# PSUM tiles of one bank from the experts on, and a new order of splits, scans and decodings

## The chip, the cores and the metric

The kernel runs on one core of a Trainium2 chip. The metric is the device time of one execution in microseconds (us), the median of three runs. The profile is of one more execution, taken by the hardware profiler. TensorE (PE) multiplies, VectorE (DVE), ScalarE (ACT) and GpSimd (POOL) do the rest, SyncE (SP) issues most of the loads. Each engine takes its instructions strictly in the order of the program and waits at an instruction until what it needs is there.

## The reference

Three layers follow each other on 2 x 768 tokens of width 512 (attention has 8 heads of 64).

```python
# 1 linear attention with decay
for t in range(S):
    state = gamma * state + einsum('bhd,bhe->bhde', k[:, :, t], v[:, :, t])
    y[:, :, t] = scale * einsum('bhd,bhde->bhe', q[:, :, t], state)
# 2 mixture of 8 experts, 512 -> 1024 -> 512
fresh_e = argmax(logits[b, s])
e = fresh_e if s == 0 or local_gate[b, s] < 0.5 else prev_e
out[b, s] = softmax(logits[b, s])[e] * (maximum(x[b, s] @ w1[e], 0) @ w2[e])
# 3 feed-forward with a convolution of three taps along the tokens
h = maximum(x @ w_in, 0)
conv_out = sum of conv_w[k] * (h shifted by k - 1)
out = (h * sigmoid(conv_out)) @ w_out
```

The weights of the third layer arrive as 64-bit floats, two 32-bit words each.

## The kernel before

The program is in the order in which the code emits it (a manual schedule); nothing sorts it afterwards. Waits between engines are set by tile: an instruction that writes into a tile waits until the earlier readers of that tile are done, whichever part of it they read.

**PSUM.** Eight banks of 128 x 512 floats. `xp`, `sc` and `x` are tiles of two banks each, `rt` and `state` of one. From the experts on the banks are handed out in rings: ring a is the two halves of `xp`, ring b the two halves of `sc` and then `rt`, ring c the two halves of `x`. `bank(ring)` gives the next one.

**Attention** works on 12 tiles of 128 tokens. Step i runs a_Z, a_AV(i), a_S(i+1) (scores, L335, masked by VectorE in L340), a_U, a_X(i) (L394, the output and the router's logits) and a_store. Spread between these are: the parts of the router, `route(g)` for five groups of tiles (codes turned by L454, a scan over tokens in L456 that holds the previous expert, back transposes in L463, counts in L470, slots in L496); the splitting of the first weights, and the decoding of the first weights of the third layer.

**Splitting.** A weight tile of 128 x 1024 (`raw`) is split in two parts, whose sum is exact: ScalarE copies it to a short type (`whi`, L174, split_first) and VectorE takes the difference (`wlo`, L182, split_second). Each product is then three matmuls: hi x hi, lo x hi, hi x lo. `split_unit` does both halves.

**Decoding.** `draw` is half a weight tile of 64-bit words. dec_load issues its DMA, dec_first lets ScalarE read it twice (L214, L215), then five VectorE operations (L217 to L223) and two of GpSimd (L225, L226) make `wdec`; dec_part runs one of these stages, dec_second all that are left, and then issues the next load.

**Experts.** Expert 0 and 7 are done in two halves of 128 tokens by `alone(e, half)` (L641 first product, ScalarE's relu `hr` L652, transposes back in L629, L660 second product, `ys` out by L670 and L671). Experts 1 to 6 are done with 256 tokens at once: L1 (L694) fills four banks (two of `sc`, `rt`, `state`) in four rounds dt; in the last round each bank, once full, is read by ScalarE (`hh`, L699) and by VectorE (`hl`, L700). T (L572) transposes the tokens of the next expert into ring a, read by ScalarE (`xsh`) and VectorE (`xsl`, L575); L2 (L723) is the second product. Between the two halves of expert 0 stands `overflow`, a branch (L816) that all engines read.

**Third layer.** c_T (L929) transposes the experts' output, six tiles a batch. h2 (L972) makes 32 blocks of 386 columns, which ScalarE reads as `hs` (L986); three taps in L989 and L991, the gate in L995 to L1001 (`gh`, `gl`). o2 (L1024) is the last product, copied out as `os` (L1038, L1047).

Of the kernel before, what the change touches and what calls it, by code (L numbers as in the profile page):

```python
# [8 lines left out]
F32 = mybir.dt.float32  # L9
# [5 lines left out]
ALU = mybir.AluOpType  # L15
AX = mybir.AxisListType
# [7 lines left out]
P = 128  # L24
# [16 lines left out]
Z_LT_HALF = -1.5 * 2.0 ** -23  # L41

WBUFS = 10
DEC_STEPS = (8, 10)
RAW_STEP = 2
SPLIT_STEPS = (4, 5, 6, 7, 8, 9, 10, 11)


def _float_of(bits):
# [51 lines left out]
def tile_kernel(ctx: ExitStack, tc: tile.TileContext, consts, qk, kv, w1, w2, w_in, conv_w, w_out, out):  # L101
# [15 lines left out]
    xrow = scr[0:YROW, :]  # L117

    psp = ctx.enter_context(tc.tile_pool(name="psp", bufs=1, space=PSUM))
    xp2, sc2, x2 = (psp.tile([P, 2, 512], F32, name=n) for n in ("xp", "sc", "x"))  # L120
    rtb, std = (psp.tile([P, 512], F32, name=n) for n in ("rt", "state"))
    rings = {"a": [xp2[:, 0], xp2[:, 1]], "b": [sc2[:, 0], sc2[:, 1], rtb], "c": [x2[:, 0], x2[:, 1]]}

    def bank(ring):
        rings[ring].append(rings[ring].pop(0))
        return rings[ring][-1]
# [119 lines left out]
    def dec_first(pool=None):  # L246
        dec_second()
        u = dnx["run"]
        if u >= len(dec_src):
            return  # L250
        dnx["run"] += 1
        dec_raw["g"] = decode(dec_raw.pop(u), wdec[u // 2][:, (u % 2) * DM:(u % 2 + 1) * DM], pool)
        next(dec_raw["g"])

    def dec_part():
        if "g" in dec_raw and next(dec_raw["g"], 0) == 0:
            dec_raw.pop("g")
            dec_load()

    def dec_second(queue=nc.sync):  # L260
        if "g" in dec_raw:
            for _ in dec_raw.pop("g"):
                pass
            dec_load(queue)
# [62 lines left out]
    def a_S(i, ps=range(NP)):  # L327

        if ps[0] == 0:
            sc_t[i] = sc2  # L330
        sc = sc_t[i]
        for p in ps:
            for j in range(2):
                o = j * D
                nc.tensor.matmul(sc[:, j, p * P:(p + 1) * P], lhsT=qk_t[i][o:o + D, p // 2, 1, p % 2, :],  # L335
                                 rhs=qk_t[i][o:o + D, p // 2, 0, p % 2, :], start=True, stop=True)
        if ps[-1] < NP - 1:
            return
        A_t[i] = at.tile([P, 2 * NP, P], F32, name="A", tag="A", bufs=1)
        nc.vector.tensor_tensor(out=A_t[i], in0=sc.rearrange("p j (a t) -> p (j a) t", a=NP),  # L340
                                in1=cv("mask").unsqueeze(1).to_broadcast([P, 2 * NP, P]), op=ALU.mult)
# [3 lines left out]
    def a_Z(i):  # L345

        xp = xp_t[i] = xp2
        if i % NC:
            z = Z[(i % NC - 1) % 2]
            for p in range(NP):  # L350
                for j in range(2):
                    o, a = slice(j * D, (j + 1) * D), slice(p % 2 * D, (p % 2 + 1) * D)
                    nc.tensor.matmul(xp[a, j, p // 2 * P:(p // 2 + 1) * P], lhsT=z[o, p * D:(p + 1) * D],
                                     rhs=qk_t[i][o, p // 2, 0, p % 2, :], start=(p < 2), stop=False,
                                     skip_group_check=True)
# [32 lines left out]
    def a_X(i):  # L388

        xT = xT_t.pop(i)  # L390
        x_t[i] = x2[:, 0], x2[:, 1]
        for p in range(NP):
            o = (p % 2) * P
            nc.tensor.matmul(x_t[i][p // 2][:, o:o + XN], lhsT=xT[:, p, :], rhs=xw[:, p, :],  # L394
                             start=(p % 2 == 0), stop=(p % 2 == 1), skip_group_check=True)
# [28 lines left out]

    def logits(i):

        nc.vector.tensor_reduce(out=LG[:, i, :], in_=x2[:, :, P:XN].rearrange("p m e -> p e m"), axis=AX.X, op=ALU.add)

    def route(g):

# [76 lines left out]
    def part(i):  # L507
        if i in rts:
            next(rts[i], None)
# [69 lines left out]
    def first_gather():  # L579

        st = st_t["st"][:, NP * D:NP * D + 4 * E]
        ve = nc.vector
        ve.tensor_copy(perm, st[:, 0:2 * E])
        ve.tensor_tensor(out=perm0, in0=perm[:, 0:1], in1=st[:, 2 * E:2 * E + 1], op=ALU.add)
        nc.gpsimd.indirect_dma_start(out=x0, out_offset=None, in_=scr[0:1 + FIRST * P, :],
                                     in_offset=bass.IndirectOffsetOnAxis(ap=perm0, axis=0))

    def first_T():
        xs0[:] = [dp.tile([P, KD, P], F32R, name="xs0", tag=tag) for tag in ("ds", "df")]
        transposed(x0, *xs0)  # L590

    def moe(mo):
# [141 lines left out]

        first = alone(0, 0, False)
        g3, g4 = len(GROUPS) - 2, len(GROUPS) - 1
        part(g3)
        rts[g4] = route(g4)
        part(g4)
        next(first)  # L740
        next(first)
        part(g4)
        next(first)
# [12 lines left out]
        for n, _ in enumerate(first):  # L756
            if n in (1, 4):
                next(blocks, None)
            if n in (3, 5):
                split_unit(nc.vector)  # L760
            if n >= 5:
                next(rest, None)
            if n == 5:
                T(0, (1,))
# [309 lines left out]
    with tc.manual_schedule():  # L1074
        a_load_qk(0, 2)
        nc.scalar.dma_start(out=tq.rearrange("p a n -> p (a n)"), in_=consts[:, 0:n0])
        nc.scalar.dma_start(out=C, in_=consts[:, n0:])
        a_load_kv(0)
        a_load_qk(1)
        a_load_kv(1)  # L1080
        a_load_qk(2)
        a_load_kv(2)
        nc.vector.memset(x_last, 0.0)
        keep_warm(10)
        nc.vector.memset(small_zero, 0.0)
        nc.gpsimd.memset(ones, 1.0)
        sloti = x0.bitcast(I32)[:, 0:CAP]
        nc.gpsimd.iota(sloti, pattern=[[1, CAP]], base=1, channel_multiplier=0)
        nc.gpsimd.tensor_copy(slot1, sloti)
        for half in range(2):  # L1090
            a_scale_q(0, nc.vector, slice(half, half + 1))
            a_S(0, range(NP)[half * NP // 2:(half + 1) * NP // 2])
        a_scale_v(0, nc.gpsimd)
        a_scale_q(1, nc.vector)
        nc.sync.dma_start(out=scr[0:1, :], in_=x_last[0:1].rearrange("p a t -> p (a t)"))
        for i in range(NT):
            if i == 0:
                gate = C[:, n_wg:n_wg + KD * (E + 1)].rearrange("p (k e) -> p k e", k=KD)
                for odd in range(2):
                    o = (E + 1) * odd  # L1100
                    nc.gpsimd.tensor_copy(xw[:, odd::2, o:o + P], ident.unsqueeze(1).to_broadcast([P, KD // 2, P]))
                    o = P if odd == 0 else 0
                    nc.gpsimd.tensor_copy(xw[:, odd::2, o:o + E + 1], gate[:, odd::2, :])
                nc.gpsimd.tensor_copy(tri, cv("mask"))
                nc.gpsimd.tensor_copy(sel, ident[:, P - 1:P].to_broadcast([P, P]))
                a_scale_v(1, nc.gpsimd)
            ends = {b: g for g, (a, b) in enumerate(GROUPS)}
            late, due, done = ends.get(i - 1), ends.get(i), ends.get(i + 1)
            a_Z(i)
            part(late)  # L1110
            a_AV(i)
            a_load_qk(i + 3)
            a_scale_q(i + 2, nc.gpsimd)
            part(late)
            if i + 1 < NT:
                a_S(i + 1)
            dec_part()
            a_U(i)
            a_load_kv(i + 3)
            a_scale_v(i + 2, nc.gpsimd)  # L1120
            dec_part()
            part(due)
            if i in SPLIT_STEPS:
                split_first()
            if i == NT - 1:
                first_T()
                part(due)
            part(late)
            if i == FIRST + 1:
                first_gather()  # L1130
            a_X(i)
            logits(i)
            a_store(i)
            if done is not None and i < NT - 1:
                rts[done] = route(done)
                part(done)
            dec_part()
            if i == DEC_STEPS[0] - 2:
                dec_load()
                dec_load()  # L1140
            if i in DEC_STEPS:
                dec_first()
            if RAW_STEP <= i and nxt["load"] < 4:
                load_unit()
            if i in SPLIT_STEPS:
                split_second(nc.vector)
        att.close()
        with ExitStack() as c2:
            mo = c2.enter_context(tc.tile_pool(name="mo", bufs=1))
            moe(mo)  # L1150
        dst.close()
        with ExitStack() as c3:
            fo = c3.enter_context(tc.tile_pool(name="fo", bufs=1))
            moe2(fo)
# [34 lines left out]
```

## Time and profile before

| | |
|---|---|
| median of three runs | 500.0 us (498.72 to 502.33) |
| profiled execution | 500.29 us |
| its span on the core | 498.5 us, 1.8 us less |
| mean granted clock of TensorE | 0.938 |

The profile's page lists the busy time of each engine, then groups of instructions. The list of waits gives for TensorE, by line, what it waited for, in us over the span, how often, and the longest. A timeline row has the start and the length of an instruction or a run of like ones, and in brackets the idle time of its engine ahead of it with what ended that. The table of stretches has the busy time of each engine between two times. A granted clock of 1.00 is 2.4 GHz, and 0.50 is 1.2 GHz.

### The profile page before, as it was taken

What the parts mean: (1) busy time and instruction counts of PE and PEld (TensorE: products, weight loads), DVE (VectorE), ACT (ScalarE), POOL (GpSimd) and SP (SyncE); (2) the same over time, 40 slices, a digit from 0 to 9 for tenths busy, and PEclk for the clock granted to TensorE, in tenths of its full rate; (3) what the DMA queues carried; (4) which work ended last, traced back from release to release, by engine and by line L of the source; (5) the groups of instructions that cost most, each with busy time, mean ns of one, the idle gap of its engine ahead of it and who ended that gap; (6) DMA issues with size and microseconds to landing.
All of it is one profiled execution on the core that took longest, in us unless ns stands there. A gap on an engine that the chain in (4) does not pass through costs nothing. (4 is left out here: it accounts for less than half of the span.)

```text
span 498.5 us, 7286 instructions
## 1 busy us (share of the span) xinstructions
PE 425.0 (85%) x2772; PEld 361.7 (73%) x2772; DVE 293.6 (59%) x484; ACT 243.5 (49%) x445; POOL 169.2 (34%) x142
## 2 busy tenths in 40 slices
PE   7998677789797896969798859868898979998996
PEld 4887565568686795968778747648886858986875
DVE  3478685628695665757556653556980632893250
ACT  2455451337463465555536441556863523773241
POOL 4544442301436072453616061603840200441020
PEclk9999877979998799999889997969999998999999
DMA  8999754536678376675928120311301001000101
GB/s 322 309 352 409 281 186 149 149 107 227 218 237 307 99 263 207 223 268 178 316 99 279 59 86 0 113 36 43 107 0 43 21 21 44 1 0 21 43 0 63
DMA packets 27718, 73.36 MB, mean 147 GB/s; under 512 B 2837, under 2 KB 3221, under 8 KB 27682
## 3 DMA queue, kind: packets, MB, share of 16 engines
q1 hardware_dynamic: 17634, 48.37, 27.4%
q0 software_dynamic: 4000, 13.66, 9.4%
q10 hardware_dynamic: 6048, 10.85, 5.8%
q8 instruction: 22, 0.36, 0.3%
q14 instruction: 14, 0.11, 0.1%
HBM read 62.39 MB, written 10.49 MB: 146 GB/s over the span
## 5 line engine op out<-in xcount | busy, mean ns | idle before, releaser
L182 DVE TENSOR_TENSOR wlo<-raw,whi 128x1024 fp32r<-128x1024 f32 x64 | 84.7, 1335 | 39.7 <-ACT whi L174 39.7
L174 ACT CAST whi<-raw 128x1024 fp32r<-128x1024 f32 x64 | 66.4, 1051 | 38.3 <-PE x L723 24.3
L996 POOL TENSOR_TENSOR sg<-sg,hs 128x384 f32<-128x384 f32 x32 | 35.4, 1105 | 114.6 <-ACT sg L995 114.5
L991 DVE SCALAR_TENSOR_TENSOR cs<-hs,cw,cs 128x384 f32<-128x384 f32 x64 | 48.2, 753 | 43.0 <-ACT cs L989 41.7
L225 POOL TENSOR_TENSOR dmf<-dmf,ds 128x512 f32<-128x512 f32 x14 | 28.1, 2008 | 127.4 <-DVE ds L223 93.6
L972 PE MATMUL sc<-x,whi 128*128 128x386 f32 x168 | 38.2, 349 | 6.4 <-ACT hs L986 6.4
L1024 PE MATMUL x<-whi,gh 128*128 128x512 f32 x88 | 36.4, 413 | 6.9 <-ACT os L1038 6.9
L694 PE MATMUL sc<-xsh,whi 128*128 128x256 f32 x96 | 28.1, 292 | 14.2 <-DVE hl L700 14.2
L723 PE MATMUL x<-whi,hh 128*128 128x512 f32 x96 | 39.0, 407 | 0.0
L723 PE MATMUL x<-wlo,hh 128*128 128x512 f32 x96 | 38.4, 400 | 0.0
L972 PEld LDWEIGHTS sc<-x,whi 128*128 128x128 f32 x168 | 30.1, 193 | 9.4 <-ACT hs L986 9.3
L1024 PE MATMUL x<-whi,gl 128*128 128x512 f32 x88 | 35.3, 402 | 0.0
L1024 PE MATMUL x<-wlo,gh 128*128 128x512 f32 x88 | 35.3, 401 | 0.0
L1001 DVE TENSOR_TENSOR gl<-sg,gh 128x384 fp32r<-128x384 f32 x32 | 29.2, 911 | 4.6 <-ACT gh L1000 4.6
L723 PE MATMUL x<-whi,hl 128*128 128x512 f32 x96 | 30.1, 395 | 0.0
L694 PEld LDWEIGHTS sc<-xsh,whi 128*128 128x128 f32 x96 | 18.6, 194 | 15.7 <-DVE hl L700 15.4
L226 POOL TENSOR_TENSOR wdec<-dmf 128x512 f32<-128x512 f32 x14 | 28.7, 2049 | 1.1
L694 PE MATMUL sc<-xsh,wlo 128*128 128x256 f32 x96 | 27.4, 286 | 0.0
L694 PE MATMUL sc<-xsl,whi 128*128 128x256 f32 x96 | 27.4, 285 | 0.0
L1024 PEld LDWEIGHTS x<-whi,gh 128*128 128x128 f32 x88 | 16.9, 192 | 13.0 <-ACT os L1038 9.6
L600 POOL DMA_INDIRECT xg<-scr,permi x15 | 18.2, 1214 | 20.6 <-DVE up L523 11.0
L340 DVE TENSOR_TENSOR A<-sc,C 128x1024 f32<-128x1024 f32 x12 | 14.7, 1223 | 13.5 <-PE sc L335 13.5
(217 smaller groups left out, 1055.1 us busy)
## 6 DMA issues: line engine op xcount, KB each, us to landing
raw<-in_moe_w_dram SPq DMA_DIRECT2D x64, 512.0 KB, 4.6
kv<-in_kv_dram SPq DMA_DIRECT2D x12, 512.0 KB, 7.3
qk<-in_qk_dram SPq DMA_DIRECT2D x11, 512.0 KB, 6.9
scr<-ys ACTq DMA_DIRECT2D x16, 256.0 KB, 5.6
draw<-in_moe_w_out_dram POOLq DMA_DIRECT2D x8, 512.0 KB, 5.0
scr<-xo ACTq DMA_DIRECT2D x11, 256.0 KB, 6.5
out_dram<-os ACTq DMA_DIRECT2D x11, 256.0 KB, 2.0
draw<-in_moe_w_in_dram SPq DMA_DIRECT2D x4, 512.0 KB, 7.3
```

Source lines behind the costliest of these rows:

```text
L174: nc.scalar.copy(hi, raw[u])
L182: engine.tensor_tensor(out=lo, in0=t, in1=hi.bitcast(F32), op=ALU.subtract)
L225: nc.gpsimd.tensor_tensor(out=f, in0=f, in1=s.bitcast(F32), op=ALU.mult)
L226: nc.gpsimd.tensor_tensor(out=out, in0=f, in1=a.bitcast(F32), op=ALU.add)
L600: nc.gpsimd.indirect_dma_start(out=t, out_offset=None, in_=xrow, in_offset=bass.IndirectOffsetOnAxis(ap=permi[:, col:col + 1], axis=0))
L694: nc.tensor.matmul(o, lhsT=a[:, fs], rhs=b_[:, dt, :], start=(dt == 0 and n == 0 and ft % 2 == 0), stop=(dt == KD - 1 and n == 2), skip_gr ...
L723: nc.tensor.matmul(yp[t], lhsT=a[:, ft, t * P:(t + 1) * P], rhs=b_[:, ws], start=(ft == 0 and a is hh and b_ is wh), stop=(ft == KF - 1 an ...
L972: nc.tensor.matmul(pb[:, 0:WN], lhsT=split[u_in + dt][wi][:, fs], rhs=x_[dt // 2][:, dt % 2, :], start=(n == 0), stop=(n == 3 * KD - 1))
L991: nc.vector.scalar_tensor_tensor(out=cs, in0=tap[j], scalar=cw[:, j, ft:ft + 1], in1=cs, op0=ALU.mult, op1=ALU.add)
L996: nc.gpsimd.tensor_tensor(out=sg, in0=sg, in1=tap[1], op=ALU.mult)
L1001: nc.vector.tensor_tensor(out=gl, in0=sg, in1=gh.bitcast(F32), op=ALU.subtract)
L1024: nc.tensor.matmul(ops[t][:, 0:n_], lhsT=a[:, ts_], rhs=b_[:, ws], start=(ft == 0 and n == 0), stop=(ft == KF - 1 and n == 2))
```

## The change

Tiles of two banks live in a pool of their own until the last attention step; then that pool is closed, and another with six tiles of one bank each is opened, from which the rings take `a0`, `a1`, `b0`, `b1` (and `rt`), `c0`, `c1`. X of the last attention tile is the first to write there, so its logits are a copy and an addition. Only unit 0 is decoded within attention, with its load issued at the end of step 7 in place of 6; unit 1 is decoded in alone(0,0). Tile 9 has no split any more, which alone(0,0) takes over, and at steps with no due route part VectorE's half of the split comes ahead of the router's logits. Code transposes and scan of a route group stand right behind S, back transposes and comparisons after X, counts after the next AV. The route of the last group begins in the last attention step, and the first transposes of the experts come behind X(11).

```diff
-DEC_STEPS = (8, 10)
+DEC_STEPS = (8,)
-SPLIT_STEPS = (4, 5, 6, 7, 8, 9, 10, 11)
+SPLIT_STEPS = (4, 5, 6, 7, 8, 10, 11)
...
-    xp2, sc2, x2 = (psp.tile([P, 2, 512], F32, name=n) for n in ("xp", "sc", "x"))
     rtb, std = (psp.tile([P, 512], F32, name=n) for n in ("rt", "state"))
-    rings = {"a": [xp2[:, 0], xp2[:, 1]], "b": [sc2[:, 0], sc2[:, 1], rtb], "c": [x2[:, 0], x2[:, 1]]}
+    pst = ExitStack()
+    psa = pst.enter_context(tc.tile_pool(name="psa", bufs=1, space=PSUM))
+    xp2, sc2, x2 = (psa.tile([P, 2, 512], F32, name=n) for n in ("xp", "sc", "x"))
+    rings = {}
...
-        x_t[i] = x2[:, 0], x2[:, 1]
+        x_t[i] = (x2[:, 0], x2[:, 1]) if i < NT - 1 else (bank("c"), bank("c"))
...
+        else:
+            nc.vector.tensor_copy(LG[:, i, :], x_t[i][0][:, P:XN])
+            nc.vector.tensor_tensor(out=LG[:, i, :], in0=x_t[i][1][:, P:XN], in1=LG[:, i, :], op=ALU.add)
...
         g3, g4 = len(GROUPS) - 2, len(GROUPS) - 1
+        next(first)
         part(g3)
-        rts[g4] = route(g4)
-        part(g4)
-        next(first)
         next(first)
...
-            if n in (3, 5):
+            if n == 2:
+                dec_first()
+            if n == 6:
+                dec_second()
+            if n in (0, 3, 5):
                 split_unit(nc.vector)
...
             a_Z(i)
-            part(late)
             a_AV(i)
             a_load_qk(i + 3)
             a_scale_q(i + 2, nc.gpsimd)
             part(late)
-            if i + 1 < NT:
+            if not last_tile:
                 a_S(i + 1)
+            part(due)
             dec_part()
             a_U(i)
             a_load_kv(i + 3)
             a_scale_v(i + 2, nc.gpsimd)
-            dec_part()
-            part(due)
+            if late is not None and due is None:
+                part(late)
+            if i == FIRST + 1:
+                first_gather()
             if i in SPLIT_STEPS:
                 split_first()
-            if i == NT - 1:
-                first_T()
-                part(due)
-            part(late)
-            if i == FIRST + 1:
-                first_gather()
+                if due is None:
+                    split_second(nc.vector)
+            if last_tile:
+                pst.close()
+                ps = ctx.enter_context(tc.tile_pool(name="ps", bufs=1, space=PSUM))
+                for n, ring in enumerate("abc"):
+                    rings[ring] = [ps.tile([P, 512], F32, name=f"{ring}{j}") for j in range(2)]
+                rings["b"].append(rtb)
             a_X(i)
             logits(i)
             a_store(i)
-            if done is not None and i < NT - 1:
+            if done is not None:
                 rts[done] = route(done)
                 part(done)
+            part(due)
+            if last_tile:
+                first_T()
             dec_part()
-            if i == DEC_STEPS[0] - 2:
+            if i == DEC_STEPS[0] - 1:
                 dec_load()
                 dec_load()
```

Three places show what moves. On TensorE, at the end of L1 of expert 3, T for expert 4 and the start of L2, with the semaphores that an instruction waits for. Before:

```order
L694 MATMUL state<-xsl,whi 128x256
L572 MATMUL xp<-C,xg 128x128 [waits DMASW4_49]
L572 MATMUL xp<-C,xg 128x128 x3
L572 MATMUL xp<-C,xg 128x128 [waits DMASW5_49,DVE_49]
L572 MATMUL xp<-C,xg 128x128 x3
L723 MATMUL x<-whi,hh 128x512 [waits Activation_49]
```

and after:

```order
L700 MATMUL state<-xsl,whi 128x256
L578 MATMUL a_982<-C,xg 128x128 [waits DMASW4_49]
L578 MATMUL a_982<-C,xg 128x128 x3
L578 MATMUL a_981<-C,xg 128x128 [waits DMASW5_49]
L578 MATMUL a_981<-C,xg 128x128 x3
L729 MATMUL c_986<-whi,hh 128x512 [waits Activation_49]
```

The order is the same; the second group of transposes no longer waits for VectorE, only for its own load.

On SP, the loads issued in steps 6 to 8 of attention. Before:

```order
L302 DMA qk<-in_qk_dram 128x1024
L309 DMA kv<-in_kv_dram 128x1024
L243 DMA draw<-in_moe_w_in_dram 128x1024 x2
L165 DMA raw<-in_moe_w_dram 128x2x512
L302 DMA qk<-in_qk_dram 128x1024
L309 DMA kv<-in_kv_dram 128x1024
```

and after:

```order
L304 DMA qk<-in_qk_dram 128x1024
L311 DMA kv<-in_kv_dram 128x1024
L167 DMA raw<-in_moe_w_dram 128x2x512
L304 DMA qk<-in_qk_dram 128x1024
L311 DMA kv<-in_kv_dram 128x1024
L167 DMA raw<-in_moe_w_dram 128x2x512
L245 DMA draw<-in_moe_w_in_dram 128x1024 x2
```

The two draws, ahead of a raw tile and of qk and kv of tile 10 before, stand behind these and the next raw tile after.

On VectorE, steps 8 and 9 of attention (`A` is the masked scores of tile 9, `far` the scan of the third group). Before:

```order
L182 TENSOR_TENSOR wlo<-raw,whi 128x1024
L340 TENSOR_TENSOR A<-sc,C 128x1024
L217 TENSOR_SCALAR dmag<-dmag 128x512
L218 TENSOR_SCALAR dmag<-dmag 128x512
L220 TENSOR_SCALAR ds<-draw 128x512
L221 SCALAR_TENSOR_TENSOR dmag<-dmag,ds 128x512
L223 TENSOR_SCALAR ds<-dmag 128x512
L456 SCALAR_TENSOR_TENSOR far<-C,far,rt 1x384
L427 TENSOR_REDUCE LG<-x 128x9
```

and after:

```order
L342 TENSOR_TENSOR A<-sc,C 128x1024
L462 SCALAR_TENSOR_TENSOR far<-C,far,rt 1x384
L219 TENSOR_SCALAR dmag<-dmag 128x512
L220 TENSOR_SCALAR dmag<-dmag 128x512
L430 TENSOR_REDUCE LG<-x 128x9
L471 TENSOR_SCALAR mi<-rt 128x3
L472 TENSOR_TENSOR OH<-mi,C 128x24
L473 TENSOR_TENSOR OHT<-OH,C 128x24
L222 TENSOR_SCALAR ds<-draw 128x512
L223 SCALAR_TENSOR_TENSOR dmag<-dmag,ds 128x512
L225 TENSOR_SCALAR ds<-dmag 128x512
```

The scan moved ahead of the decoding, whose last three operations moved behind the logits and the comparisons of the route.

## Rows read from the trace of the kernel before

**Rows 1.** The page's first part: busy time, share of the span, instructions.

```profile
PE 425.0 (85%) x2772; PEld 361.7 (73%) x2772; DVE 293.6 (59%) x484; ACT 243.5 (49%) x445; POOL 169.2 (34%) x142
```

**Rows 2.** Waits of TensorE: line, what it waited for, us, times, longest.

```profile
PE sc L694 <- DVE hl L700: 14.2, 6, 3.5
PE xp L572 <- DVE xsl L575: 9.1, 6, 1.6
PE x L1024 <- ACT os L1038: 6.9, 7, 2.3
PE sc L972 <- ACT hs L986: 6.4, 9, 1.3
PE sc L641 <- ACT hr L652: 6.0, 2, 5.4
PE xp L929 <- DVE x L942: 5.4, 5, 1.5
...
PE sc L641 <- ACTq L816: 2.8, 1, 2.8
```

**Rows 3.** Timeline of one wait in expert 4, all engines.

```profile
215.50 1.23 DVE L182 TENSOR_TENSOR wlo<-raw,whi 128x1024 fp32r<-128x1024 f32 x1 [1.65 <-ACT whi L174]
...
216.64 0.68 DVE L700 SCALAR_TENSOR_TENSOR hl<-sc,hh 128x512 fp32r<-128x512 f32 x1
...
217.38 0.39 PE L694 MATMUL sc<-xsh,whi 128*128 128x256 f32 x1 [2.28 <-DVE hl L700]
```

**Rows 4.** Stretches: alone(0,1), experts, c_T and h2, o2, h2.

```profile
core 0: us, PE busy (x) PEld busy (x) DVE busy (x) ACT busy (x) POOL busy (x), PEclk, DMA share, GB/s
100.00:106.00 6.00, 5.40 (x13) 4.25 (x14) 0.00 (x0) 0.00 (x0) 0.94 (x1) 0.50 0.45 132
158.00:168.00 10.00, 8.12 (x32) 7.24 (x33) 4.23 (x7) 4.29 (x7) 0.67 (x1) 0.50 0.38 134
189.73:217.38 27.65, 23.79 (x152) 21.43 (x153) 18.27 (x24) 15.02 (x20) 12.50 (x9) 1.00 0.68 229
248.00:253.00 5.00, 3.60 (x14) 2.82 (x13) 2.18 (x5) 2.71 (x4) 0.00 (x0) 0.50 0.31 117
321.00:336.00 15.00, 9.59 (x40) 6.59 (x40) 8.81 (x20) 7.88 (x19) 2.54 (x3) 0.75 0.24 68
328.80:338.00 9.20, 7.54 (x24) 5.96 (x25) 4.43 (x9) 4.13 (x10) 0.00 (x0) 0.50 0.00 1
410.50:413.70 3.20, 3.20 (x8) 2.52 (x9) 0.00 (x0) 0.00 (x0) 0.00 (x0) 0.50 0.24 84
423.96:445.62 21.66, 19.79 (x108) 18.84 (x108) 18.85 (x27) 17.20 (x36) 9.39 (x9) 1.00 0.00 1
```

**Rows 5.** Timeline of ScalarE at loads that are decoded, experts 2 and 7.

```profile
154.43 0.66 ACT L214 ACTIVATE dmf<-draw 128x512 f32<-128x512 f32 x1 [4.84 <-DMA draw<-in_moe_w_in_dram]
...
296.48 0.66 ACT L214 ACTIVATE dmf<-draw 128x512 f32<-128x512 f32 x1 [2.98 <-DMA draw<-in_moe_w_out_dram]
```

**Rows 6.** Attention from step 6 on: timeline, and the page's row of such loads.

```profile
39.05 1.87 SPq L243 DMA_DIRECT2D draw<-in_moe_w_in_dram  x2
...
43.76 0.42 SPq L302 DMA_DIRECT2D qk<-in_qk_dram  x1
...
55.02 1.76 PE L335 MATMUL sc<-qk 64*128 64x128 f32 x16 [2.17 <-POOL qk L316]
...
57.96 0.42 DVE L217 TENSOR_SCALAR dmag<-dmag 128x512 f32<-128x512 f32 x1
...
62.07 0.99 DVE L456 TENSOR_TENSOR_SCAN far<-C,far,rt 1x384 f32<-1x384 f32 x1
...
63.12 0.48 PE L463 MATMUL rt<-C,far 1*128 1x1 f32 x3 [2.83 <-DVE far L456]
...
76.21 0.37 PE L463 MATMUL rt<-C,far 1*128 1x1 f32 x2 [1.20 <-DVE far L456]
draw<-in_moe_w_in_dram SPq DMA_DIRECT2D x4, 512.0 KB, 7.3
```

More of the change, by code (lines that the diff above doesn't have):

```diff
@@ L425, in logits @@
     def logits(i):
-        nc.vector.tensor_reduce(out=LG[:, i, :], in_=x2[:, :, P:XN].rearrange("p m e -> p e m"), axis=AX.X, op=ALU.add)
+        if i < NT - 1:
+            nc.vector.tensor_reduce(out=LG[:, i, :], in_=x2[:, :, P:XN].rearrange("p m e -> p e m"), axis=AX.X, op=ALU.add)
+        else:
+            nc.vector.tensor_copy(LG[:, i, :], x_t[i][0][:, P:XN])
+            nc.vector.tensor_tensor(out=LG[:, i, :], in0=x_t[i][1][:, P:XN], in1=LG[:, i, :], op=ALU.add)
     def route(g):
@@ L1108, in tile_kernel @@
             late, due, done = ends.get(i - 1), ends.get(i), ends.get(i + 1)
+            last_tile = i == NT - 1
             a_Z(i)
-            part(late)
             a_AV(i)
```

## The prediction

> **What bounds the kernel now.** I read the busy totals first. TensorE is busy 425.0 us of the 498.5 [rows 1], so a saving must come from its 73 idle us or from time at the lower clock. The waits of TensorE come second, because they say what the idle time was for: the six longest lines of the list are waits for readers of PSUM, 14.2 us in L1 (L694), 9.1 us in T (L572), 6.9 us in o2 (L1024), 6.4 us in h2 (L972), 6.0 us in alone (L641) and 5.4 us in c_T (L929), 48.0 us in all [rows 2]. The third view is the timeline of one such wait [rows 3]. VectorE first finishes a low part of the weights begun at 215.50, its read of the first bank of ring b starts at 216.64 and lasts 0.68, and at 217.38 TensorE starts matmuls that had waited 2.28 us. Those matmuls go to the other bank of the tile `sc`. Nothing in the computation asks for that wait; the two banks merely belong to one tile. The fourth view is the table of stretches [rows 4]: from one such start to the next an expert takes 27.65 us, of which TensorE is busy 23.79, VectorE 18.27, ScalarE 15.02 and GpSimd 12.50, at a clock of 1.00. TensorE sets the pace there, with 3.86 us of idle time in each expert.
>
> The clock adds to it. After the longest stalls the granted clock stands at 0.50, the lower level of 1.2 GHz: 158 to 168 (behind a stall of 3.5 us, the longest of the L694 line), 100 to 106, 248 to 253, 328.8 to 338 and 410.5 to 413.7 [rows 4]. Half of TensorE's busy time in such a stretch is what the level costs.
>
> **Experts (one-bank tiles).** After the change `sc<-xsh,whi` into the second bank, and the transposes into the second bank of ring a, wait for the readers of their own bank alone, a ring's turn older. That takes away 14.2 and 9.1 us. For the clock I take half of 8.12 us (158 to 168) and of 3.60 us (248 to 253), 4.1 + 1.8 = 5.9 us; the second stretch follows an ordinary stall and may be less, so 5.5. What is late next? The same VectorE read is wanted only by the hl matmuls of L2. Ahead of those stand the rest of the last L1 round (18 matmuls; an expert has 96 of 256 columns and 48 of 512, which are 192 of the small kind, so 23.79 / 192 = 0.12 us each and 2.2 us), T and four matmuls of L2, together about 4 us, against the 2.28 that it was late. So it is covered. The engines would then have 18.27 us of VectorE in a period of about 23.8. Sum -28.8; between -15 and -32.
>
> **Second FFN.** h2 loses 6.4 us of waits for the hs copy of the bank just filled, and o2 loses 6.9 for os copies of the other bank, plus half of 3.20 us at the low clock behind the longest of those, which is 2.3 us [rows 2, 4]. In a stretch of nine h2 blocks VectorE is busy 18.85 of 21.66 us and TensorE 19.79 [rows 4], so VectorE is close behind. I give back 1 us for lag at the ends of h2, where drain waits for the last blocks. Sum -13.9, between -7 and -16.
>
> **c_T, between experts and second FFN.** 5.4 us of waits, and half of 7.54 us at the low clock, 3.8, would be 9.2. But from 321 to 336 VectorE is busy 8.81 us and ScalarE 7.88 [rows 4], working in turn on one tile, so TensorE can't pass through in under about 9: at most -6.2. I take -5.5, with bounds -2 and -6.2.
>
> **alone(7,0).** 5.39 of the 6.0 us at L641 are one stall, for the hr read that ScalarE reached late: it had itself waited 2.98 us for a weight tile to be decoded (its row at 296.48) [rows 5]. With ring b in own tiles the next group of matmuls starts at once, but the transposes a few matmuls later still want hr. Only six matmuls of 512 columns go ahead, at twice 0.12 us: -1.4. Bounds 0 and -4.
>
> **alone(0,0) and alone(0,1).** The rest of the L641 line, 0.6, goes. The 2.8 us wait for ScalarE's branch event also stood on ring b's other bank; it now stands twelve matmuls later. With half of 5.40 us at the low clock (100 to 106) that is 0.6 + 2.8 + 2.7 = 6.1 us. Against it stands the moved decoding of unit 1: five VectorE operations ahead of the final copies of alone(0,0), behind which ScalarE's ys copy, its DMA and the branch are queued, so alone(0,1) waits. Its price is bounded by the decoding's length before, 57.96 to 62.07, 4.1 us, with other work between [rows 6], and by zero. I take 1.5, and 0.9 back for smaller waits in this stretch that the later split_units prevent. Sum -5.5, between 0 and -8.
>
> **Attention, steps 8 to 11.** Before, the scan (L456, 62.07) stood behind the decoding that started at 57.96 on VectorE, and TensorE waited 2.83 us for it at 63.12, and 1.20 us once more at 76.21 [rows 6]. Now the scan is ahead of the decoding's VectorE part, and the back transposes sit behind X. That is -4.0. S(10) waited 2.17 us at 55.02 for its qk tile, which was queued on SP at 43.76 behind two draws of 39.05 and a raw tile; draws now come behind qk(10), kv(10) and the raw tile, so 2.2 goes too. What the draws lose: they land 7.3 us after issue at the median [rows 6], ScalarE reaches its first operation on them (L214) in order and stands there, and the xT copies of tile 9 are queued behind it. I price that at +2.8 (bounds 0 and 5, the longest such wait being 4.84, at 154.43 [rows 5]). The first split goes from tile 9 to alone(0,0), where both engines have gaps: no cost. Logits of the last tile take two VectorE operations instead of one, hidden behind the last low part. Counts once after AV: no cost. Less stalling should win 1.5 of the low clock and some 1 us of the last tile's chain. Sum -4.0 - 2.2 + 2.8 - 2.5 = -5.9, between +1 and -8. Closing the first PSUM pool makes X(11) wait for readers that are all older than its own input: nothing.
>
> **Sum.** -28.8 - 13.9 - 5.5 - 1.4 - 5.5 - 5.9 = -61.0. The profiled execution took 500.3 us, 1.8 us outside its span, and stands 0.3 above the median of 500.0. So 439 us. The bounds added up give -25 to -74, but they won't all fall on one side: 429 to 449 is this case's own range.
>
> **Rivals.**
> *VectorE becomes the bound.* Removing the false waits packs its work closer: in h2 18.85 of 19.79 us are 95%, and experts would hold 18.27 of 23.8. For: the operations come in order behind ScalarE's, so any late one delays the next block. Against: blocks may lag across the three banks of the ring, and o2 gives VectorE time to catch up. It would keep half of the experts' and of h2's gain, 15 of 28.8 and 7 of 13.9: 439 + 22 = 461. The Trainium skill ("SBUF — State Buffer", section "Who interferes with whom") says that a VectorE operation with two inputs in SBUF contends with GpSimd when that one reads SBUF, whoever issues later being blocked. By that rule closer packing makes VectorE's operations themselves longer, which is one more way into this case and not a price of its own.
>
> *The tail of attention keeps its time.* ScalarE's stand at the later draws costs the full 4.84 twice, and the moved decoding its full 4.1; both terms vanish, 439 + 11.4 = 450.
>
> *The change does not do what it says.* If waits were kept by the pool's space and not by tile, only the reordering would show: 500 - 11 = 489. Against: the order of after shows transposes of the second half without the VectorE wait.
>
> *Slower, by the clock.* Suppose TensorE now pauses briefly at each bank in experts and second FFN and the clock drops to its lower level for most of it. Each us of full-clock work at the lower level costs one more. The gain of 61 is eaten when 61 us of work beyond what is at the lower level now run there; half of the experts' work (six times 23.79 is 143) would cost 71, and 439 + 71 = 510. Against: two expert periods ran at 1.00 although each had 3.86 us of idle time [rows 4], and the change takes idle time away. The Trainium skill ("TensorE: Matmul & The Clock Gate", section "A second HAM failure mode: psum-queue depth-cycling") describes such a kernel: rotation through banks with small idles between groups, and a clock that swings between its two levels. Row 189.73 of the table speaks against that here.
>
> **How the numbers follow.** Forecast 0.62, VectorE 0.16, tail 0.14, no effect 0.03, clock 0.02, other 0.03. The range 428 to 462 holds nearly nine tenths of the forecast, the tail case and half of the VectorE case, 0.8. About 1% is what a measurement of this kernel can tell from no change; every case but the clock and part of the rest is faster by more: 0.96 faster, 0.02 same, 0.02 slower.
>
> **What would show it.** Of TensorE's waits the lines of L694 for hl, L572 for xsl and L1024 for os should be gone or under 1 us each; the expert period 24 us at 1.00 and no stretch of an expert at 0.50; h2 at 2.2 us a block with VectorE above 93%; c_T from 321 to 336 shortened to about 9.5. the waits of rows 55.02, 63.12 and 76.21 should be gone, and a new wait for ScalarE's xT at tile 9 of about 3 us should be seen. The forecast is wrong if waits for hl in L2 take the place of the old ones, or if ScalarE's waits for draws grow in the experts: these loads have 3.9 us less time in each period.

## The result: 438.8 us, and the profile after

The changed kernel takes 438.84 us (median of four runs, 436.1 to 440.16). The ratio to the kernel before is 0.8817, with a 95% interval of 0.872 to 0.892; the kernel before, run beside it, took 499.36 us. Ratios leave out slow runs, those over 1.5% above the fastest of their kernel; medians take in all runs. The forecast was 439. The profiled execution was the fastest of the four: 436.1 us, with a span of 434.3.

The page's first line on engines and the waits of TensorE after (line, cause, us, times, longest) answer to [rows 1] and [rows 2]. L1 is now L700, T L578, o2 L1032, h2 L980, alone L647, c_T L937.

```profile
PE 402.2 (93%) x2772; PEld 348.1 (80%) x2772; DVE 293.3 (68%) x485; ACT 241.5 (56%) x445; POOL 171.0 (39%) x142
```

```profile
PE rt L647 <- ACTq L824: 4.7, 1, 4.7
PE a L635 <- ACT hr L658: 4.0, 1, 4.0
PE state L507 <- DVE sl L502: 2.6, 2, 1.6
PE a L937 <- ACT x L947: 2.2, 1, 2.2
PE a L578 <- DMA xg<-scr,permi: 2.0, 1, 2.0
PE rt L460 <- DVE code L456: 1.9, 2, 1.3
PE c L1032 <- ACT os L1046: 1.7, 1, 1.7
...
PE a L937 <- DVE x L950: 1.5, 2, 0.8
```

VectorE and ScalarE are as busy as before, 293 and 242 us. The waits for hl, xsl and hs, 29.7 us before, are not in the list any more, and o2 keeps 1.7 of its 6.9. TensorE itself is 23 us less busy with the same 2772 matmuls, and its mean granted clock rose from 0.938 to 0.980. The stretches after show where (columns as in [rows 4]). The last stretch but three is a period of an expert, the last one is h2 alone.

```profile
core 0: us, PE busy (x) PEld busy (x) DVE busy (x) ACT busy (x) POOL busy (x), PEclk, DMA share, GB/s
97.90:103.90 6.00, 5.82 (x16) 4.71 (x17) 2.35 (x3) 4.26 (x6) 0.09 (x1) 0.52 0.47 154
111.10:250.87 139.77, 139.77 (x914) 128.39 (x913) 115.76 (x148) 89.27 (x120) 69.47 (x45) 1.00 0.76 258
204.28:227.57 23.29, 23.29 (x153) 21.40 (x152) 17.81 (x25) 14.92 (x20) 12.15 (x9) 1.00 0.80 269
278.89:289.93 11.04, 7.12 (x40) 4.81 (x40) 7.97 (x19) 6.88 (x19) 2.54 (x3) 1.00 0.32 92
289.93:434.30 144.37, 139.02 (x723) 124.74 (x721) 82.97 (x126) 80.92 (x168) 44.03 (x38) 1.00 0.10 35
368.00:388.00 20.00, 20.00 (x116) 20.00 (x114) 18.90 (x26) 16.72 (x35) 10.06 (x9) 1.00 0.00 1
```

Through the whole of experts 1 to 6, 139.77 us, TensorE has not one recorded gap and its clock stays at 2.4 GHz. Before, the same stretch took 172.12 us with 148.80 busy, at 0.95:

```profile
118.66:290.78 172.12, 148.80 (x913) 133.83 (x912) 117.32 (x148) 90.06 (x120) 69.90 (x45) 0.95 0.61 208
```

The nine profiles in this document with one-bank tiles in all three rings have 139.8 to 142.4 us for these experts.

The start of the first matmul of each stage divides the span. The table has the length of each stage in us, worked out from these starts in the timelines; "alone(0)" is alone(0,0) and alone(0,1) with the branch between.

| kernel | attention | alone(0) | experts 1-6 | alone(7) | c_T | rest |
|---|---|---|---|---|---|---|
| before | 79.8 | 38.9 | 172.1 | 30.2 | 15.0 | 162.5 |
| after | 73.5 | 37.6 | 139.8 | 28.0 | 11.0 | 144.4 |
| forecast of the difference | -5.9 | -5.5 | -28.8 | -1.4 | -5.5 | -13.9 |
| measured difference | -6.3 | -1.2 | -32.4 | -2.2 | -3.9 | -18.2 |

The total hides errors that cancel: too much was expected of alone(0) and c_T, too little of the experts and the rest. The measured differences add up to -64.2, the forecast ones to -61.0; the profiled execution after is 2.7 us under the median of its kernel. What stands against alone(0) is one chain. This is the timeline from the decoding of unit 1 to the branch, without the rows of TensorE's steady work:

```profile
89.75 0.42 DVE L219 TENSOR_SCALAR dmag<-dmag 128x512 f32<-128x512 f32 x1
...
91.72 0.43 DVE L225 TENSOR_SCALAR ds<-dmag 128x512 int32<-128x512 int32 x1
...
92.33 1.28 POOL L227 TENSOR_TENSOR df<-df,ds 128x512 f32<-128x512 f32 x1 [6.42 <-DVE dif L556]
92.34 1.29 DVE L557 TENSOR_TENSOR dif<-dif,isov 128x12 f32<-128x12 f32 x1
...
93.69 1.28 POOL L228 TENSOR_TENSOR wdec<-df,dmag 128x512 f32<-128x512 f32 x1
93.76 1.32 DVE L561 TENSOR_TENSOR ex<-LG,MX 128x96 f32<-128x96 f32 x1
...
96.14 0.36 DVE L676 COPY ys<-c 128x256 f32<-128x256 f32 x1
...
96.53 0.37 ACT L677 COPY ys<-c 128x256 f32<-128x256 f32 x1 [1.13 <-DVE ys L676]
...
98.08 0.79 PE L647 MATMUL rt<-whi,xsh 128*128 128x512 f32 x1 [4.71 <-ACTq L824]
```

The five operations of the decoding hold VectorE 2.4 us, from 89.75 to 92.15. Then two small operations that took 0.17 and 0.25 us before take 1.29 and 1.32, while the two GpSimd operations of the same decoding run. VectorE's copy of ys is queued behind these, ScalarE's copy waits for it, the branch stands behind that, and TensorE stands 4.7 us and then runs at a clock of 0.52 for 6 us.

### The profile page after: what moved, and what is told of

It reads as the page before. It is cut to its first block, busy times and chain, and to the rows that moved or that the text cites. A ratio compares the mean times of both kernels' runs of the same rounds, so it can differ in the third digit from the quotient of the medians.

```text
span 434.3 us, 7275 instructions
## 1 busy us (share of the span) xinstructions
PE 402.2 (93%) x2772; PEld 348.1 (80%) x2772; DVE 293.3 (68%) x485; ACT 241.5 (56%) x445; POOL 171.0 (39%) x142
## 5 line engine op out<-in xcount | busy, mean ns | idle before, releaser
L1004 POOL TENSOR_TENSOR sg<-sg,hs 128x384 f32<-128x384 f32 x32 | 37.4, 1169 | 92.2 <-ACT sg L1003 92.1
L729 PE MATMUL c<-whi,hh 128*128 128x512 f32 x96 | 37.9, 395 | 0.0
L729 PE MATMUL c<-wlo,hh 128*128 128x512 f32 x96 | 37.4, 389 | 0.0
L1032 PE MATMUL c<-whi,gh 128*128 128x512 f32 x88 | 35.2, 399 | 1.7 <-ACT os L1046 1.7
L980 PE MATMUL b<-x,whi 128*128 128x386 f32 x168 | 35.5, 340 | 0.0
L1032 PE MATMUL c<-whi,gl 128*128 128x512 f32 x88 | 35.0, 397 | 0.1
L1032 PE MATMUL c<-wlo,gh 128*128 128x512 f32 x88 | 34.7, 395 | 0.0
L980 PEld LDWEIGHTS b<-x,whi 128*128 128x128 f32 x168 | 29.6, 189 | 0.8 <-ACT hs L994 0.7
L729 PE MATMUL c<-whi,hl 128*128 128x512 f32 x96 | 29.6, 389 | 0.0
L700 PE MATMUL b<-xsl,whi 128*128 128x256 f32 x96 | 27.2, 283 | 0.0
L700 PE MATMUL b<-xsh,wlo 128*128 128x256 f32 x96 | 27.2, 283 | 0.0
L700 PE MATMUL b<-xsh,whi 128*128 128x256 f32 x96 | 27.1, 283 | 0.0
L1003 ACT ACTIVATE sg<-cs 128x384 f32<-128x384 f32 x32 | 16.7, 522 | 14.4 <-DVE gl L1009 14.4
```

The lines of the kernel that those rows point to most:

```text
L700: nc.tensor.matmul(o, lhsT=a[:, fs], rhs=b_[:, dt, :], start=(dt == 0 and n == 0 and ft % 2 == 0), stop=(dt == KD - 1 and n == 2), skip_gr ...
L729: nc.tensor.matmul(yp[t], lhsT=a[:, ft, t * P:(t + 1) * P], rhs=b_[:, ws], start=(ft == 0 and a is hh and b_ is wh), stop=(ft == KF - 1 an ...
L980: nc.tensor.matmul(pb[:, 0:WN], lhsT=split[u_in + dt][wi][:, fs], rhs=x_[dt // 2][:, dt % 2, :], start=(n == 0), stop=(n == 3 * KD - 1))
L1004: nc.gpsimd.tensor_tensor(out=sg, in0=sg, in1=tap[1], op=ALU.mult)
L1032: nc.tensor.matmul(ops[t][:, 0:n_], lhsT=a[:, ts_], rhs=b_[:, ws], start=(ft == 0 and n == 0), stop=(ft == KF - 1 and n == 2))
```

## The experiments

My theory was that waits set by the two-bank tiles are some 55 of the 61 us, and the new order the rest; the rival, that the new order relieves VectorE and ScalarE and the tiles only show their lateness. Ratios are to the kernel before, run on the same chip, with 95% intervals.

**Each half of the change alone.** First the new order with the old tiles:

```diff
+    xp2, sc2, x2 = (psp.tile([P, 2, 512], F32, name=n) for n in ("xp", "sc", "x"))
     rtb, std = (psp.tile([P, 512], F32, name=n) for n in ("rt", "state"))
-    pst = ExitStack()
-    psa = pst.enter_context(tc.tile_pool(name="psa", bufs=1, space=PSUM))
-    xp2, sc2, x2 = (psa.tile([P, 2, 512], F32, name=n) for n in ("xp", "sc", "x"))
-    rings = {}
+    rings = {"a": [xp2[:, 0], xp2[:, 1]], "b": [sc2[:, 0], sc2[:, 1], rtb], "c": [x2[:, 0], x2[:, 1]]}
...
-            if last_tile:
-                pst.close()
...
```

> The changed order of splits, scans, counts and decodings, with the three two-bank PSUM tiles kept to the end. Theory (the waits set by two-bank tiles are some 55 of the 61 us): about 491 us, the waits of TensorE for hl (L1, 14 us), xsl (T, 9 us), os (7 us) and hs (6 us) stand as before, only the time up to alone(0,0) is some 6 us shorter. Rival (the new order is what relieves VectorE and ScalarE, and the tiles matter little): 470 us or less, with the hl and xsl waits halved.

Measured: 501.02 us, ratio 0.9998 (0.996 to 1.004). The waits of TensorE for hl, xsl, os and hs stand as before, and the one behind the branch has grown:

```profile
PE sc L694 <- DVE hl L700: 13.6, 6, 3.1
PE xp L572 <- DVE xsl L575: 9.1, 6, 1.6
PE sc L641 <- ACTq L818: 7.7, 1, 7.7
PE x L1026 <- ACT os L1040: 6.9, 7, 2.3
PE sc L974 <- ACT hs L988: 6.4, 9, 1.3
```

The new order alone is worth nothing. Attention is 2.7 us shorter (77.1), and alone(0) 5.3 longer (44.1 against 38.9): the wait behind the branch is 7.7 us in place of 2.8 [rows 2]. Each of the other stages is within 2.0 us of before.

Then the new tiles with the old order:

```diff
...
             if i == NT - 1:
+                pst.close()
+                ps = ctx.enter_context(tc.tile_pool(name="ps", bufs=1, space=PSUM))
+                for n, ring in enumerate("abc"):
+                    rings[ring] = [ps.tile([P, 512], F32, name=f"{ring}{j}") for j in range(2)]
+                rings["b"].append(rtb)
                 first_T()
```

> The order of before, with tiles of one bank each opened ahead of the last attention tile's first transposes. Theory: about 447 us, experts at 23.3 us a period without idle time of TensorE, attention as long as before (alone(0,0) starts at about 79.5 us). Rival: 465 us or more, hl or xsl waits remaining in the experts since the old order delays VectorE.

Measured: 438.85 us, ratio 0.8787 (0.873 to 0.884). That is the gain of the whole change within the intervals, and 8 us better than my theory had it. Attention takes 80.7 us, as before; alone(0) takes 32.0, 5.6 us less than in the changed kernel, since the wait behind the branch is 0.7:

```profile
PE rt L647 <- ACTq L822: 0.7, 1, 0.7
```

So the theory of the tiles holds more strictly than I had it, and the rival falls. What the new order wins in attention it pays in alone(0): against the old tiles 2.7 us won and 5.3 paid, in one profile each.

**Ring by ring.** The changed kernel with one-bank tiles for one ring, the other two rings in tiles of two banks in the same pool:

```diff
                 for n, ring in enumerate("abc"):
-                    rings[ring] = [ps.tile([P, 512], F32, name=f"{ring}{j}") for j in range(2)]
+                    if ring == "a":
+                        rings[ring] = [ps.tile([P, 512], F32, name=f"{ring}{j}") for j in range(2)]
+                    else:
+                        two = ps.tile([P, 2, 512], F32, name=f"{ring}2")
+                        rings[ring] = [two[:, 0], two[:, 1]]
```

> The changed order, with one-bank tiles for ring a alone (transposes of T, alone and c_T); rings b and c stay tiles of two banks. Theory (each ring's false waits are a saving of their own): against the reordered kernel with all two-bank tiles (about 491 us) minus 9 for T and minus 4 for c_T, about 478 us; the hl waits of L1 stay at 14 us. Rival (VectorE's lateness is the cause and the tiles only show it): the hl waits grow by what the xsl waits lose, about 489 us.

> The changed order, with one-bank tiles for ring b alone (L1, h2, first product of alone). Theory: about 491 minus 14 (hl), minus 6 (hs), minus 7 of low clock behind those stalls, about 464 us; the xsl waits of T stay at 9 us. Rival: the xsl waits grow, about 475 us or more.

> The changed order, with one-bank tiles for ring c alone (second products, o2). Theory: about 491 minus 7 (os), minus 2 of low clock, about 482 us, all of it in the third layer. Rival: no change against 491, since ScalarE and VectorE are behind in o2 anyway.

| one-bank tiles for | us | ratio | experts 1-6 | c_T | rest |
|---|---|---|---|---|---|
| none (the order alone) | 501.0 | 0.9998 | 170.1 | 15.3 | 163.5 |
| ring a | 484.3 | 0.970 (0.960 to 0.980) | 163.5 | 11.7 | 161.0 |
| ring b | 474.6 | 0.949 (0.938 to 0.961) | 162.3 | 15.4 | 153.2 |
| ring c | 493.7 | 0.988 (0.979 to 0.997) | 172.1 | 15.0 | 153.7 |
| all (after) | 438.8 | 0.882 (0.872 to 0.892) | 139.8 | 11.0 | 144.4 |

My expectations counted from 491 for the order alone, which took 501.0. By the ratios ring a saves some 15 us against it (13 expected), ring b 25 (27) and ring c 6 (9). The hl waits stayed with ring a, as the theory had it; the xsl waits grew with ring b, as the rival had it.

In the rest, ring a saves 2.5 us against the order alone, ring b 10.3 and ring c 9.8, and all three 19.1: this nearly adds up. c_T is ring a's alone. In the experts the savings do not add up: ring a saves 6.7 and ring b 7.8, ring c nothing, and all three 30.4. (Rings a and b without c were not run; the matmuls into ring c there, L2, have no wait in the list of any of these runs.) The waits of TensorE say why. With ring a alone,

```profile
PE b L700 <- DVE hl L706: 14.4, 6, 3.4
```

and with ring b alone

```profile
PE a L578 <- DVE xsl L581: 13.2, 6, 2.8
```

With ring a the wait in T is gone, and the wait in L1 as long as before. With ring b the wait in L1 is gone, and TensorE comes to T sooner; VectorE's xsl is sooner by less, so the 9.1 us there have become 13.2. In the last of the six experts, counted from the start of the last round of L1, T begins at 2.88 us in place of 5.42, and its second group at 5.55 in place of 7.59; the wait between grows from 1.57 to 2.07. To that extent the rival is right: VectorE is late by 1.4 to 3.4 us in each expert, and a tile moves that lateness from one wait to the next. Where neither wait is asked for, it costs nothing. The second cause is the clock. The experts' stretch with ring a, with ring b, and one of ring b's six waits with a stretch right behind it:

```profile
115.74:279.19 163.45, 149.04 (x913) 136.41 (x912) 117.52 (x148) 90.25 (x120) 68.48 (x45) 0.95 0.66 221
```

```profile
116.28:278.61 162.33, 149.13 (x914) 134.02 (x912) 115.67 (x148) 89.01 (x120) 68.18 (x45) 0.95 0.67 221
265.59 0.66 PE L578 MATMUL a<-C,xg 128*128 128x128 f32 x4 [2.07 <-DVE xsl L581]
266.50:271.50 5.00, 5.00 (x16) 3.92 (x16) 1.92 (x2) 2.19 (x3) 0.00 (x0) 0.66 0.01 3
```

With one kind of wait left, TensorE is busy 149 us, as before; with both gone 139.8. The 9 us of the clock come back only with the last of these stalls. The rest of the difference is the wait that is left: 163.45 - 149.04 = 14.4 and 162.33 - 149.13 = 13.2 us.

**The order's loss in alone(0).** Unit 1's decoding moved once more, behind the branch:

```diff
-            if n == 2:
-                dec_first()
-            if n == 6:
-                dec_second()
...
         for n, _ in enumerate(alone(0, 1, True)):
-            if n == 4:
+            if n == 0:
+                dec_first()
+            elif n == 2:
+                dec_second()
+            elif n == 4:
                 dec_first(mo)
```

> The changed kernel with the decoding of unit 1 moved once more, from alone(0,0) to the steps behind the branch in alone(0,1). Theory (the decoding and the GpSimd operations that run beside VectorE's small ones hold back the copies of alone(0,0), and so the branch): the wait of 4.7 us behind the branch falls under 2 us, the stretch at the low clock that followed it goes, alone(0,0) and alone(0,1) together take 32 us in place of 37.6, and the time is 433 us. Rival (the branch itself and the DMA ahead of it are the wait): 437 to 439 us, the wait stays above 3.5 us.

Measured: 435.13 us, ratio 0.8683 (0.864 to 0.873); the wait for ACTq is not in the list any more, and alone(0) takes 34.6 us. The two operations of VectorE that had taken 1.29 and 1.32 us take 0.17 and 0.25 again. The interval of the ratio meets that of the changed kernel, so both ran again on one chip:

> The changed kernel unaltered, as the measure for the three runs beside it. About 438.5 us; the stretch up to alone(0,0) between 73.5 and 76.5 us, which is how far the runs with this order lie apart so far.

> The kernel of the late decoding of unit 1 once more, on the same chip as the changed kernel. Theory (the decoding ahead of the branch costs what the new order wins in attention): 3 to 5 us under the changed kernel run beside it. Rival (the first difference was chance): within 1.5 us of it.

Measured: the changed kernel 440.73 us (437.57 to 443.97, ratio 0.885, 0.878 to 0.891), the late decoding 436.44 (430.36 to 437.72, ratio 0.866, 0.855 to 0.878). By the medians that is 4.3 us less, within what the theory gave; by the ratios, which here rest on three of its six runs, some 9. The size is open between these, the sign is not. alone(0) takes 32.2 us against 37.4, and its second half runs at 1.00:

```profile
93.64:107.81 14.17, 13.60 (x64) 10.52 (x65) 11.10 (x19) 10.79 (x17) 6.24 (x4) 1.00 0.63 206
```

The place of that decoding ahead of the branch is what the new order pays in alone(0).

**The loads to be decoded, one step earlier.** `dec_load` at `DEC_STEPS[0] - 2` again, the rest as changed.

> The changed kernel with the two loads to be decoded issued one step earlier, as before. Theory (the later issue costs ScalarE next to nothing and spares the scores of tile 10 their late operand): alone(0,0) starts 1.5 to 2.5 us later than in the changed kernel, with a wait of some 2 us of TensorE for qk in step 9, 440 to 441 us. Rival (the later issue only trades one wait for another): no difference, 438 to 439 us.

Measured: 437.74 us, ratio 0.878 (0.869 to 0.886), alone(0,0) starts at 75.3. The wait for qk came back with 1.3 us, but of ten other profiled executions with the new order nine start alone(0,0) anywhere from 73.6 to 77.1 (and one at 79.6), so the 1.8 us to the changed kernel's profile say nothing. The rival holds: no difference can be told.

**The wait in alone(7,0).** First only the decoding begun later there, from n == 2 to n == 5:

> The changed kernel with the decoding that starts in alone(7,0) begun three steps later, behind ScalarE's first relu there. Theory (ScalarE stands at a load to be decoded, and the relu is queued behind it): TensorE's wait of 4.0 us for hr falls under 1 us, the time is 435 us. Rival (the relu waits for GpSimd to free its buffer, whatever the order): the wait stays above 2.5 us and the time at 438 us.

Measured: 443.96 us, ratio 0.889 (0.885 to 0.893). That is no gain; whether it is slower than the changed kernel the ratios leave open, but alone(7) takes 31.2 us in place of 28.0. The first relu now comes in time, at 258.97, but the second, at 269.56, is late: TensorE waits 5.3 us for it, and ScalarE's own wait says what for:

```profile
ACT hr L658 <- POOL wdec L228: 5.2, 1, 5.2
```

My theory fell, and the rival holds in part: the relu's buffers are two that it shares with the decoding, and the later decoding now holds what the second relu wants. So a second edit gave the relu other buffers, moved the decoding of the weights behind the second relu, and that of the convolution's weights two steps later:

```diff
-                hr[f] = mo.tile([P, 512], F32, name="hr", tag="ow", bufs=2)
+                hr[f] = mo.tile([P, 512], F32, name="hr", **(dict(tag="xg", bufs=4) if e == E - 1 else dict(tag="ow", bufs=2)))
...
-            if n == 2:
+            if n == 7:
                 dec_first(mo)
-            if n == 9:
+            if n == 11:
                 dec_second(nc.gpsimd)
-            if n == 4:
+            if n == 6:
...
-            if n == 10:
+            if n == 13:
                 cwp = bank("a")
```

> The changed kernel with ScalarE's relu of alone(7) in buffers that it shares with the gathered tokens in place of the decoding's, and the decoding in alone(7,0) begun behind the second relu, that of the convolution's weights behind the last product of the first stage. Theory (two things held the relu: the load that ScalarE stands at, and the buffer that GpSimd frees; moving the decoding alone left the second): TensorE's wait of 4.0 us for hr goes under 1 us, about 3 us less than the changed kernel. Rival (the wait moves to the decoded weights, which alone(7,1) splits): no difference.

Measured: 436.51 us, ratio 0.875 (0.869 to 0.882), beside 440.73 for the changed kernel. The intervals of the ratios overlap, so the total is less sure than the stage: the wait for hr is 0.9 us, alone(7) takes 24.4 us against 27.4, and c_T 1.0 us more. (That the moved decoding now meets c_T would explain this, but no run shows it. The profiled execution was the longest of the six, 442.35 us; the next kernel has 24.3 for alone(7) in a faster one.)

> Both together: late decoding of unit 1 and the relu's own buffers. Theory: the two savings are in different stages and add up, about 432 us, 6 to 8 us under the changed kernel run beside it. Rival: one of them alone, 435 us.

Measured: 431.99 us (430.05 to 433.14), ratio 0.866 (0.860 to 0.872). All of its runs lie under all of the changed kernel's beside it; by the medians it is 8.7 us less. alone(0) takes 31.0 us and alone(7) 24.3, so both savings are there. Its ratio can't be told from that of the late decoding alone.

```profile
247.67:271.98 24.31, 21.60 (x99) 16.46 (x98) 15.90 (x26) 11.66 (x20) 13.43 (x12) 1.00 0.23 70
```

## Why the prediction was right, and where its terms were not

**Experts.** The mechanism held: the waits went, VectorE's hl read was covered, and nothing took their place in this profile (1.5 us for hh in L2 in one of the others). -28.8 was forecast and -32.4 measured. The waits gave the 23.3 us that were in the list. The term mis-sized was the clock: 5.5 from two stretches, 148.80 - 139.77 = 9.0 measured. I took only the two stretches that I had found behind long stalls; the mean of 0.95 over the 172 us could have been read from the trace before, and would have given 0.05 x 172 = 8.6.

**Second FFN.** Forecast -13.9, measured -18.2. The waits fell from 13.3 to 1.7 us, and TensorE's busy time from 145.1 to 139.0, 6.1 us, where I had taken 1.6 from one stretch and given 1.0 back for lag. VectorE does run at the edge (18.90 of 20.0 us in h2) but holds up no block in that stretch. The rival that made VectorE the bound named a real quantity that isn't reached. The Trainium skill ("SBUF — State Buffer", section "Who interferes with whom") has a VectorE operation with two SBUF inputs contend with a GpSimd operation that reads SBUF; the two small operations of 1.29 and 1.32 us in alone(0) agree. But that effect cost time there, ahead of a branch; in the experts VectorE was busy 117.3 us before and from 115.2 to 122.8 in the nine profiles with one-bank tiles, and the whole stage differed by 2.6 us between these.

**c_T.** Forecast -5.5, measured -3.9. The step "TensorE can't pass through in under about 9" was right in kind: two waits of 2.2 and 1.5 us on ScalarE and VectorE are left and the clock is 1.00. It was too hopeful in size. The two engines work in turn, 7.97 + 6.88 us of partly serial work in 11.04; that this sets the length is argued, and no run tests it.

**alone(7,0).** -1.4 and -2.2: six matmuls go ahead and the wait is 4.0 instead of 5.4, as worked out. The step that named the load as its cause was the larger part: in the changed kernel ScalarE stands 3.05 us at the load and then 0.63 at the buffer shared with the decoding:

```profile
256.64 0.67 ACT L216 ACTIVATE dmf<-draw 128x512 f32<-128x512 f32 x1 [3.05 <-DMA draw<-in_moe_w_out_dram]
...
258.49 0.60 ACT L658 ACTIVATE hr<-b 128x512 f32<-128x512 f32 x1 [0.63 <-POOL wdec L228]
```

Where the load alone was taken out of its way, the buffer held the second relu for 5.2.

**alone(0).** Forecast -5.5, measured -1.2. The step that failed is the price of the moved decoding. I took 1.5 with an upper bound of 4.1, from the decoding's own length. Kernels without it there take 32.0 (the tiles alone) and 34.6, 32.2 and 31.0 (the late decoding, the last with the relu's buffers), so it costs about 5 of the 37.6 us, between 3.0 and 6.6. VectorE's 2.4 us for it and 2.2 for two operations stretched beside GpSimd (1.29 + 1.32 - 0.17 - 0.25) come near the stall of 4.7, and a stretch at 0.52 follows; that the decoding is the cause is shown by moving it, how its cost divides is argued. The gain of 6.1 that the tiles should bring there was right: 38.9 - 32.0 = 6.9.

**Attention.** -5.9 against -6.3 looks right, but its profile is the shortest of those taken; the ten others with this order have a mean of 75.8 against 79.8 and 80.7 in the two with the old order, so about -4.5. That the term came out so near is luck. ScalarE's stand at the later loads, +2.8 in my sum, was 0.4 us, and the wait of about 3 us for xT that I named as a sign did not come: TensorE's two waits for it are 0.8 us together. The scan's waits went, as forecast, and in part came back as waits for sl and code (2.6 and 1.9 us).

**The sum by its halves.** My terms credit the order with 5.3 us net (5.9 in attention, less 1.5 and plus 0.9 in alone(0)), and the rival of no effect even with 11. No gain from it can be told: 0.9998 alone, and 438.85 without it against 438.84 with it. The forecast of 439 came within 0.2 us by luck, since the clock gave 8 us more than I took in the experts and the second FFN, and alone(0) and c_T gave 5.9 less.

**Two of my sums are off.** The bounds of the terms add up to -23 and -74, not -25; and with its own prices the tail rival leaves 1.9 us of the two terms (+1.0 in attention, -2.9 in alone(0)), so it should stand at 448.5 and not 450. The forecast does not rest on either.

**Clock.** The rival of a clock that swings with rotation through the banks did not come: 1.00 through experts and h2.

## What to carry to other kernels

Where a tile holds several banks, a wait may be for a reader of the neighbour; look in the timeline for the bank that the waiting matmul writes. Remove all such waits of a loop at once: here a late engine moved from one wait to the next, and the clock came back only with the last. A step that is moved to where engines have gaps is priced by what stands behind it up to the next branch or copy, and by what runs beside it, not by its own length.

## What the runs showed of the hardware that was not expected

- Waits of the same length are followed by different clocks in one and the same kernel. Before, TensorE waited 2.28 us for hl at 217.38 and again at 245.01. From the first on it ran at 1.00:

```profile
217.38:245.01 27.63, 23.78 (x152) 21.43 (x152) 18.28 (x24) 15.01 (x20) 12.47 (x9) 1.00 0.66 231
245.01 0.39 PE L694 MATMUL sc<-xsh,whi 128*128 128x256 f32 x1 [2.28 <-DVE hl L700]
```

  Behind the second it stood at 0.50 from 248 to 253 [rows 4]. With ring b alone, 0.66 over 5 us follows a wait of 2.07. The length of one stall does not decide it; what does is left open.
- Two operations of 128x12 and 128x96 elements, 0.17 and 0.25 us, took 1.29 and 1.32 us on VectorE and ended within 0.11 us of GpSimd operations of 1.28 us that ran beside them; with the decoding elsewhere they took 0.17 and 0.25 again.
- With neither kind of wait, TensorE ran 139.77 us without a recorded gap while VectorE was busy 115.76 us of it.
